# Copying two output banks on two engines, and moving one batch's side work to other steps, in an attention-then-MLP kernel

## The chip, the cores and the metric

The kernel runs on one core of one Trainium2 chip. The metric is the device time of one execution in microseconds; a time is given as the median of several executions.

## The reference, cut to what matters

```
def _attn_ref(q, k, v, agents):
    a2k = sm(agents, k)          # softmax over the 12480 keys, 49 agents
    agent_v = a2k @ v
    q2a = sm(q, agents)          # softmax over the 49 agents
    return q2a @ agent_v

def _moe_ref(x, w_in, w_out):
    h = x @ w_in                 # 128 -> 2048
    g = np.maximum(0.01 * h, h)  # leaky relu
    return g @ w_out             # 2048 -> 128
```

There are two batches of 12480 tokens with 128 channels, and all 24960 rows pass through the MLP.

## The kernel before, in words

The sums over the keys and values give a small matrix per batch; its product with `w_in` is folded into the tiles `m_hi` and `m_lo`, so that a token's 49 attention weights lead straight to its 2048 hidden values. The leaky relu is written as 0.99 times a relu plus a linear part, which the products with `l_hi` and `l_lo` carry. Every factor is split in a rounded high part and a low rest, to reach float32 accuracy with three products.

**Blocks and steps.** Tokens are worked in 52 blocks of 480 (26 for each batch). A block has 8 steps, f = 0 to 7, one for each pair of hidden tiles. In a step TensorE makes `mm1` (L739, 6 matmuls of 64 rows into an `h` pair of banks; there are two such pairs), ScalarE and VectorE make the relu's parts `hi` (L759) and `lo` (L760), and two steps later (`LAG`) TensorE makes `mm2` (L766, 12 matmuls) into the two output banks `o[0]` and `o[1]` of the block. Matmuls of 64 rows run in two halves of the array side by side: rows 0 to 63 go to `o[0]`, rows 64 to 127 to `o[1]`.

**The turnover.** There is one set of output banks. The last `mm2` of block i-1 stands in step f = 1 of block i, and the first one of block i in step f = 2. In between `o_copy` (L794) brings both banks to SBUF; GpSimd adds the two copies and SyncE stores the block (`o_add`, L808). `o_copy` stands at the beginning of step f = 2, ahead of that step's `mm1`.

**Side work.** Other work is hung onto steps by a table: `at(step, fn, ...)` puts a function behind the `relu` of a step, ahead of its `mm2`. Each engine works through its own instructions in the order in which the program issues them, so the table sets the queues. Two kinds matter here.

- The attention weights of a later block, by `chain` (L820): `q_half` (L614, products `aux<-qhi` and `aux<-qlo` at f = 1 and f = 2), `q_sum` at f = 0 on VectorE (tile `sm`), `q_swap` at f = 0 on GpSimd (two copies that exchange halves of `sm`), `q_rec` at f = 1 on VectorE (three instructions into `rs`, L696 to L703), `q_norm` at f = 1 on GpSimd.
- The second batch's sums, during the first batch's blocks. `k_score` and `k_keep` (scores and running maximum) at f = 5 of blocks 0 to 6; then `k_max0` to `k_max3` (the maximum over the tile, turned by TensorE and spread again); then for each half chunk of values `k_vhi` (VectorE rounds the values into `vr`), `k_vlo`, `k_ehi`, `k_elo`, and for each two of them `k_av2` (L438: 16 matmuls into a bank pair `aux`, then two VectorE additions into `avs`). There are 13 calls of `k_av2`, in blocks 9 to 21. The pair `aux` is a single buffer (`ps_x`, L140) that `k_score`, `k_max1`, `k_av2`, `q_half` and the products for `m_hi` share. At the end `fin`, `f_parts`, `w_parts`, `k_m2` and `k_m` make `m_hi` and `m_lo` of the second batch.

The main loop and the two functions that the change cuts apart are printed here.

Of the kernel before, what the change touches and what calls it, by code (L numbers as in the profile page):

```python
# [8 lines left out]
F32 = mybir.dt.float32  # L9
# [54 lines left out]
def tile_agent_attention_then_leaky_mlp(  # L64
# [27 lines left out]
    nc = tc.nc  # L92
# [7 lines left out]
    NB = G * TP  # L100
# [14 lines left out]
    LAG = 2  # L115
    NP = NF // 2
# [31 lines left out]
    def halves(name):  # L148

        return [ps_o.tile([P, MC], F32, tag=f"o{g}", name=f"{name}{g}") for g in range(2)]  # L150

    def pair(name):
        return ps_h.tile([P, 2, MC], F32, tag="h", name=name)
# [356 lines left out]
    fin = f_add, f_den, f_tr, f_avT, f_rec  # L510
# [223 lines left out]
                nc.sync.dma_start(out=t[o:o + SL], in_=t[x:x + SL])  # L734


    h_t, r_t, o_t = {}, {}, {}

    def mm1(i, p):  # L739

        b = i // BPB
        ps = pair("h")
        t = pT_t[i]
        for n, (w, x) in enumerate(((m_hi, 0), (m_hi, 1), (m_lo, 0))):
            for g, r in enumerate(ROWS):
                nc.tensor.matmul(  # L746
                    ps[:, g, :NB], lhsT=w[b][r, cols(2 * p + g)], rhs=t[r, x],
                    start=(n == 0), stop=(n == 2),
                )
        h_t[i, p] = ps  # L750

    def cols(f):
        return slice(f * P, (f + 1) * P)

    def relu(i, p):
        ps = h_t.pop((i, p))[:, :, :NB]
        hi = rp.tile([P, 2, NB], F32R, tag="hi", name="hi")
        lo = rp.tile([P, 2, NB], F32R, tag="lo", name="lo")
        nc.scalar.activation(hi, ps, AF.Relu)  # L759
        nc.vector.scalar_tensor_tensor(  # L760
            out=lo, in0=ps, scalar=0.0, in1=hi.bitcast(F32),
            op0=ALU.max, op1=ALU.subtract,
        )
        r_t[i, p] = (hi, lo)

    def mm2(i, p):  # L766

        b = i // BPB
        if p == 0:
            o_t[i] = halves("o")  # L770
        o = o_t[i]
        hi, lo = r_t.pop((i, p))

        def add(w, x, start=False, stop=False):
            for g, r in enumerate(ROWS):
                nc.tensor.matmul(o[g][:, :NB], lhsT=w[r], rhs=x[r], start=start, stop=stop)  # L776

        for g in range(2):
            f = 2 * p + g
            add(wo_hi[:, f, :], hi[:, g], start=(f == 0))  # L780
            add(wo_lo[:, f, :], hi[:, g])
        if p == NP // 2:
            t = pT_t[i]
            for w, x, g in ((l_hi, 0, 0), (l_lo, 0, 1), (l_hi, 1, 0)):
                g ^= i % 2 == 0
                r = ROWS[g]
                nc.tensor.matmul(  # L787
                    o[g][:, :NB], lhsT=w[b][r], rhs=t[r, x], start=False, stop=False
                )
        for g in range(2):  # L790
            f = 2 * p + g
            add(wo_hi[:, f, :], lo[:, g], stop=(f == NF - 1))

    def o_copy(i):  # L794
        t = p1.tile([P, 2, NB], F32, tag="oT", name="oT")
        o = o_t.pop(i)
        if i < NBLK - 1:
            for g in range(2):
                nc.scalar.copy(t[:, g], o[g][:, :NB])  # L799
            x_t["o"] = t  # L800
            return
        h = NB // 2
        for c, eng in ((slice(0, h), nc.sync), (slice(h, NB), nc.scalar)):
            nc.scalar.copy(t[:, 1, c], o[1][:, c])
            nc.vector.tensor_tensor(out=t[:, 0, c], in0=o[0][:, c], in1=t[:, 1, c], op=ALU.add)
            eng.dma_start(out=out[:, i * NB + c.start:i * NB + c.stop], in_=t[:, 0, c])
# [9 lines left out]
    def at(step, fn, *a):  # L816
        side.setdefault(step, []).append((fn, a))
# [21 lines left out]
    for b in range(1, B):  # L839
        i0 = (b - 1) * BPB  # L840

        n0 = NP * i0 + 5
        for c in range(NCH):
            s = n0 + c // 2 * NP
            if c == 0:
                at(s - 5, load_k, b, 0)
                at(s - 5, load_k, b, 1)
            if c + 2 < NCH:
                at(s - 1, load_k, b, c + 2)
            at(s, k_score, b, c, 0)  # L850
            at(s, k_score, b, c, 1)
            if c % 2:
                at(s, k_keep, b, c - 1)
            if c % 2 or c == NCH - 1:
                at(s, k_keep, b, c)
        n0 += (NCH - 1) // 2 * NP
        for p, fn in ((1, k_max0), (3, k_max1), (3, k_max1d), (7, k_max2), (7, k_max3)):
            at(n0 + p, fn, b)
        n0 += NP
        lag = 7  # L860
        for h in range(NH):
            s = n0 + h * NP // 2
            if h % 2 == 0:
                c = h // 2
                at(s - 5, load_v, b, c)
                at(s, k_sub, b, c, nc.gpsimd)
                at(s + 2, k_exp, b, c)
            at(s + 3, k_ehi, b, h, h, nc.scalar)
            at(s + 3, k_elo, b, h, h, nc.gpsimd)
            at(s + 1, k_vhi, b, h, h, nc.vector)  # L870
            at(s + 2, k_vlo, b, h, h, nc.gpsimd)
            if h % 2:
                at(s + lag, k_av2, b, h // 2)
        n0 += (NH - 1) * NP // 2 + lag
        for p, fn in zip((1, 5, 5, 5, 5), fin):
            at(n0 + p, fn, b)
        at(n0 + 7, f_parts, b)
        for m in range(0, NM, 2):
            s = n0 + 5 + (m // 2 + 1) * NP
            at(s - 4, w_parts, b, m)  # L880
            at(s - 2, w_parts, b, m + 1)
            at(s, k_m2, b, m)
        at(s + NP, k_m, b, NM)

    with tc.manual_schedule():
# [28 lines left out]
        for o, a, n in SLOTS:  # L914
            nc.vector.tensor_tensor(
                out=sel[:, o:o + n], in0=ident[:EW, a:a + n],
                in1=ident[:EW, HALF + a:HALF + a + n], op=ALU.add,
# [10 lines left out]
        for what, c in loads:  # L928
            fn, cost = fetch[what]
# [17 lines left out]
        for n in range(2 * NM):  # L947
# [11 lines left out]
            if n % 2 == 0:  # L959
                m = n // 2  # L960
# [54 lines left out]
        steps = [(i, p) for i in range(NBLK) for p in range(NP)]  # L1015
        for s in range(len(steps) + LAG):
            if s < len(steps):
                i, f = steps[s]
                if i > 0 and f == LAG:
                    o_copy(i - 1)  # L1020
                mm1(*steps[s])
                relu(*steps[s])
                for fn, a in side.get(s, ()):
                    fn(*a)
            if s >= LAG:
                mm2(*steps[s - LAG])
        o_copy(NBLK - 1)


# [37 lines left out]
```

## Time and profile before

| | |
|---|---|
| median of 3 executions | 996.9 us (996.54 to 997.06) |
| the profiled execution, its own time | 997.26 us |
| its span, first to last instruction | 995.4 us |
| TensorE matmul busy | 970.8 us, 98% |
| VectorE busy | 735.8 us, 74% |
| ScalarE busy | 616.3 us, 62% |
| GpSimd busy | 385.7 us, 39% |
| granted TensorE clock | full in all 40 slices (2.4 GHz) |

A TensorE that is busy 98% of the span isn't working 98% of it: the end of a matmul is modelled, so one that waits between two others can look like a long one. What a step costs is read from the distance between the same instruction in successive steps or blocks.

### The profile page before, as it was taken

The page shows a single profiled execution, that of the slowest core. Times are in us where ns is not written, and L with a number is a line of the kernel's source. Part 1 is how long each engine was busy: PE and PEld are TensorE (multiplying, and loading weights), DVE is VectorE, ACT ScalarE, POOL GpSimd, SP SyncE. Part 2 cuts the span into 40 slices and gives each one's busy share as a digit, 9 for nine tenths or more (in the row PEclk, how much of TensorE's full clock was granted, in tenths as well). Part 3 has the DMA queues.
Part 4 walks back from the last instruction along what each step waited for, and adds up shares of the span by engine and source line. Part 5 has one row for each costly group of instructions (what it writes and reads, how often), then busy time and mean ns, then how long its engine had stood idle before and what let it go on. Part 6 is the DMA issues. An engine that isn't in the chain of part 4 may idle for free.

```text
span 995.4 us, 23015 instructions
## 1 busy us (share of the span) xinstructions
PE 970.8 (98%) x9438; PEld 838.4 (84%) x9438; DVE 735.8 (74%) x1071; ACT 616.3 (62%) x907; POOL 385.7 (39%) x561
## 2 busy tenths in 40 slices
PE   8889999999999999999999999999999999999998
PEld 6768888888888888888888888888888888888887
DVE  7967677678778778777777677767777777777774
ACT  5755666666666656655666666666666666666654
POOL 2113233345655655653433333333333333333320
PEclk9999999999999999999999999999999999999999
DMA  9931322312312312311111111111111111212110
GB/s 347 372 119 32 111 71 90 81 51 72 81 50 71 82 51 71 81 32 51 41 30 51 41 51 40 51 41 51 41 44 47 42 50 31 60 32 61 31 40 21
DMA packets 28836, 70.01 MB, mean 70 GB/s; under 512 B 4387, under 2 KB 17955, under 8 KB 28731
## 3 DMA queue, kind: packets, MB, share of 16 engines
q1 hardware_dynamic: 28587, 68.42, 22.7%
q8 instruction: 74, 1.21, 0.5%
q14 instruction: 31, 0.25, 0.1%
q10 hardware_dynamic: 144, 0.12, 0.0%
HBM read 43.46 MB, written 12.78 MB: 57 GB/s over the span
## 4 chain that ended last, share of the span: by engine, by line
PE 89%; DVE 5%; ACT 2%; DMA 2%; issue 1%; POOL 1%; SPq 0%; DVEq 0%; POOLq 0%; ACTq 0%
PE o L776 54%; PE h L746 27%; PE aux L620 3%; DVE lo L760 2%; ACT hi L759 2%; PE o L787 1%; PE aux L353 1%; DVE avs L453 1%; PE sc L353 1%; DMA kt<-in_k_dram 1%; DMA vt<-in_v_dram 1%; PE avw L469 1%; DVE sm L688 1%; PE avw L302 0%; PE mp L535 0%
## 5 line engine op out<-in xcount | busy, mean ns | idle before, releaser
L760 DVE SCALAR_TENSOR_TENSOR lo<-h,hi 128x960 fp32r<-128x960 f32 x416 | 481.1, 1157 | 229.3 <-ACT hi L759 215.1
L759 ACT ACTIVATE hi<-h 128x960 fp32r<-128x960 f32 x416 | 405.6, 975 | 297.7 <-PE h L746 288.8
L776 PE MATMUL o<-hi,wo_hi 64*128 64x480 f32 x1664 | 426.6, 384 | 0.0
L776 PE MATMUL o<-hi,wo_lo 64*128 64x480 f32 x1664 | 413.7, 379 | 0.0
L746 PE MATMUL h<-pT,m_hi 64*128 64x480 f32 x1664 | 330.5, 377 | 1.0 <-POOL pT L319 0.8
L776 PE MATMUL o<-lo,wo_hi 64*128 64x480 f32 x1664 | 328.8, 375 | 0.0
L776 PEld LDWEIGHTS o<-hi,wo_hi 64*128 64x128 f32 x1664 | 260.1, 184 | 34.1 <-ACT oT L799 14.0
L776 PEld LDWEIGHTS o<-hi,wo_lo 64*128 64x128 f32 x1664 | 259.0, 184 | 17.7
L746 PEld LDWEIGHTS h<-pT,m_hi 64*128 64x128 f32 x1664 | 226.6, 184 | 21.1 <-POOL pT L319 1.1
L776 PEld LDWEIGHTS o<-lo,wo_hi 64*128 64x128 f32 x1664 | 227.3, 184 | 19.6
L746 PE MATMUL h<-pT,m_lo 64*128 64x480 f32 x832 | 235.3, 375 | 0.0
L746 PEld LDWEIGHTS h<-pT,m_lo 64*128 64x128 f32 x832 | 134.7, 184 | 12.7
L319 POOL TENSOR_TENSOR pT<-pt,pT 64x480 fp32r<-64x480 f32 (+1 forms) x52 | 63.6, 1223 | 147.0 <-ACT pT L722 147.0
L665 POOL COPY sm<-sm 32x15 f32<-32x15 f32 (+1 forms) x52 | 9.8, 189 | 189.0 <-DVE sm L688 189.0
L319 POOL TENSOR_TENSOR qlo<-qt,qhi 128x480 fp32r<-128x480 f32 x52 | 64.0, 1231 | 46.3 <-ACT qhi L583 45.2
L708 POOL TENSOR_TENSOR pd<-d,rs 64x375 f32<-64x375 f32 (+1 forms) x52 | 42.5, 818 | 92.1 <-DVE rs L703 86.1
L799 ACT COPY oT<-o 128x480 f32<-128x480 f32 x102 | 52.1, 563 | 29.1 <-PE o L776 29.1
L810 POOL TENSOR_TENSOR oT<-oT 128x480 f32<-128x480 f32 x51 | 62.4, 1223 | 9.8 <-issue 9.8
L319 POOL TENSOR_TENSOR d<-st,mm 64x375 f32<-64x375 f32 (+1 forms) x52 | 44.4, 854 | 49.0 <-DVE mm L671 47.8
L620 PE MATMUL aux<-qhi,a_hl 64*128 64x240 f32 x200 | 39.9, 284 | 10.1 <-DVE avs L453 8.2
L319 POOL TENSOR_TENSOR vr<-vt,vr 120x512 fp32r<-120x512 f32 x26 | 33.9, 1302 | 32.6 <-DVE vr L314 30.4
L620 PEld LDWEIGHTS aux<-qhi,a_hl 64*128 64x128 f32 x200 | 27.6, 184 | 17.5 <-issue 14.1
(139 smaller groups left out, 873.0 us busy)
## 6 DMA issues: line engine op xcount, KB each, us to landing
qt<-in_q_dram SPq DMA_DIRECT2D x53, 240.0 KB, 2.7
kt<-in_k_dram SPq DMA_DIRECT2D x26, 480.0 KB, 7.9
out_dram<-oT SPq DMA_DIRECT2D x51, 240.0 KB, 2.0
pT<-pT SPq DMA_DIRECT2D x100, 120.0 KB, 2.3
vt<-in_v_dram SPq DMA_DIRECT2D x13, 520.0 KB, 8.2
vt<-in_v_dram SPq DMA_DIRECT2D x13, 487.5 KB, 4.4
w<-in_w_in_dram SPq DMA_DIRECT2D x4, 512.0 KB, 7.3
w<-in_w_out_dram SPq DMA_DIRECT2D x4, 512.0 KB, 8.1
```

What stands on the lines that cost most here:

```text
L319: eng.tensor_tensor(out=o, in0=x, in1=y, op=ALU.subtract)
L353: nc.tensor.matmul(ps[r, j * NA:(j + 1) * NA], lhsT=k_t[b, c][:, j, r], rhs=a_sb[:, b, :], start=True, stop=True,)
L453: nc.vector.tensor_tensor(out=av_t[b], in0=ps[:EW, g, :VW], in1=av_t[b], op=ALU.add)
L469: nc.tensor.matmul(av_t[b][o:o + NA], lhsT=s_sb[:, c, j, :], rhs=v_t[b, c][:TP, j, :], start=False, stop=False,)
L620: nc.tensor.matmul(s_t[i][:, m, :h], lhsT=a_hl[i // BPB][r], rhs=x[r, m * h:(m + 1) * h], start=(s == 0 and n == 0), stop=(n == 1), skip_g ...
L708: nc.gpsimd.tensor_tensor(out=pd[:n, :, :A0], in0=d[:n], in1=w[:n].to_broadcast([n, NT, A0]), op=ALU.mult,)
L746: nc.tensor.matmul(ps[:, g, :NB], lhsT=w[b][r, cols(2 * p + g)], rhs=t[r, x], start=(n == 0), stop=(n == 2),)
L759: nc.scalar.activation(hi, ps, AF.Relu)
L760: nc.vector.scalar_tensor_tensor(out=lo, in0=ps, scalar=0.0, in1=hi.bitcast(F32), op0=ALU.max, op1=ALU.subtract,)
L776: nc.tensor.matmul(o[g][:, :NB], lhsT=w[r], rhs=x[r], start=start, stop=stop)
L799: nc.scalar.copy(t[:, g], o[g][:, :NB])
L810: nc.gpsimd.tensor_tensor(out=t[:, 0], in0=t[:, 0], in1=t[:, 1], op=ALU.add)
```

## The change

The relu is cut in two: `relu` keeps the ScalarE part, the new `rest` makes VectorE's `lo`. In seven steps of a block `rest` follows `relu` at once, as before. In step f = 1 of every block but the first (`turnover`) it comes last: after the side work and after the last `mm2` of the block before, the two output banks are copied, `o[0]` by ScalarE and `o[1]` by VectorE, and then `rest` is issued. The values of the second batch begin 6 steps later, the turned maximum (`k_max1`, `k_max1d`) one step earlier, and what closes the batch is spaced to stay at its old places within a block.

```
     def relu(i, p):
         ...
         nc.scalar.activation(hi, ps, AF.Relu)
+        r_t[i, p] = (hi, lo)
+        l_t[i, p] = ps
+
+    def rest(i, p):
+        hi, lo = r_t[i, p]
         nc.vector.scalar_tensor_tensor(
-            out=lo, in0=ps, scalar=0.0, in1=hi.bitcast(F32),
+            out=lo, in0=l_t.pop((i, p)), scalar=0.0, in1=hi.bitcast(F32),
             op0=ALU.max, op1=ALU.subtract,
         )
-        r_t[i, p] = (hi, lo)
...
         if i < NBLK - 1:
-            for g in range(2):
-                nc.scalar.copy(t[:, g], o[g][:, :NB])
+            nc.scalar.copy(t[:, 0], o[0][:, :NB])
+            nc.vector.tensor_copy(t[:, 1], o[1][:, :NB])
...
-        for p, fn in ((1, k_max0), (3, k_max1), (3, k_max1d), (7, k_max2), (7, k_max3)):
+        for p, fn in ((1, k_max0), (2, k_max1), (2, k_max1d), (7, k_max2), (7, k_max3)):
             at(n0 + p, fn, b)
-        n0 += NP
+        n0 += NP + 6
...
-        for p, fn in zip((1, 5, 5, 5, 5), fin):
+        for p, fn in zip((1, 7, 7, 7, 7), fin):
             at(n0 + p, fn, b)
-        at(n0 + 7, f_parts, b)
+        at(n0 + 9, f_parts, b)
         for m in range(0, NM, 2):
-            s = n0 + 5 + (m // 2 + 1) * NP
+            s = n0 + 7 + (m // 2 + 1) * NP
...
             if s < len(steps):
                 i, f = steps[s]
-                if i > 0 and f == LAG:
-                    o_copy(i - 1)
-                mm1(*steps[s])
-                relu(*steps[s])
+                turnover = i > 0 and f == LAG - 1
+                mm1(i, f)
+                relu(i, f)
+                if not turnover:
+                    rest(i, f)
                 for fn, a in side.get(s, ()):
                     fn(*a)
             if s >= LAG:
                 mm2(*steps[s - LAG])
+            if s < len(steps) and turnover:
+                o_copy(i - 1)
+                rest(i, f)
         o_copy(NBLK - 1)
```

Within a block `k_av2` thereby moves from f = 0 to f = 6 of the same block, `k_vhi` from f = 2 and 6 to f = 0 and 4, `k_ehi` and `k_elo` from f = 0 and 4 to f = 2 and 6, `k_sub` and `k_exp` from f = 5 and 7 to f = 3 and 5.

VectorE's queue at a turnover of the second batch's blocks, where no values are summed. Here is the order before; `sm` is made at f = 0, `rs` at f = 1, and the `lo` between them belongs to f = 1:

```order
707 L688 TENSOR_REDUCE sm<-d 64x15
708 L760 SCALAR_TENSOR_TENSOR lo<-h,hi 128x960
709 L696 SCALAR_TENSOR_TENSOR rs<-sm 64x15
710 L700 TENSOR_TENSOR rs<-rs,d 64x15
711 L703 RECIPROCAL rs<-rs 64x15
712 L760 SCALAR_TENSOR_TENSOR lo<-h,hi 128x960
713 L716 STREAM_TRANSPOSE pt<-pd 64x480
```

And the same place in the changed kernel:

```order
709 L688 TENSOR_REDUCE sm<-d 64x15
710 L696 SCALAR_TENSOR_TENSOR rs<-sm 64x15
711 L700 TENSOR_TENSOR rs<-rs,d 64x15
712 L703 RECIPROCAL rs<-rs 64x15
713 L803 COPY oT<-o_9906 128x480
714 L765 SCALAR_TENSOR_TENSOR lo<-h,hi 128x960 x2
715 L716 STREAM_TRANSPOSE pt<-pd 64x480
```

The bank's copy (L803) stands behind the three `rs` instructions and ahead of `lo` of f = 1, which has moved behind `rs` and the copy and now stands next to `lo` of f = 2.

VectorE's queue at the same place of a block in which values are summed, before (`avs` are the two additions of `k_av2`, `vr` the rounding of `k_vhi`):

```order
280 L688 TENSOR_REDUCE sm<-d 64x15
281 L453 TENSOR_TENSOR avs<-aux,avs 113x258 x2
282 L760 SCALAR_TENSOR_TENSOR lo<-h,hi 128x960
283 L696 SCALAR_TENSOR_TENSOR rs<-sm 64x15
284 L700 TENSOR_TENSOR rs<-rs,d 64x15
285 L703 RECIPROCAL rs<-rs 64x15
286 L760 SCALAR_TENSOR_TENSOR lo<-h,hi 128x960
287 L716 STREAM_TRANSPOSE pt<-pd 64x480
288 L646 TENSOR_TENSOR sq<-aux,sx 64x480
289 L314 CAST vr_114<-vt 120x4x128
```

And now:

```order
294 L453 TENSOR_TENSOR avs<-aux,avs 113x258 x2
295 L765 SCALAR_TENSOR_TENSOR lo<-h,hi 128x960 x2
296 L688 TENSOR_REDUCE sm<-d 64x15
297 L314 CAST vr_114<-vt 120x4x128
298 L696 SCALAR_TENSOR_TENSOR rs<-sm 64x15
299 L700 TENSOR_TENSOR rs<-rs,d 64x15
300 L703 RECIPROCAL rs<-rs 64x15
301 L803 COPY oT<-o_3710 128x480
302 L765 SCALAR_TENSOR_TENSOR lo<-h,hi 128x960 x2
```

The additions have left f = 0 and stand two `lo` earlier, behind `lo` of f = 6; a rounding of values has come between `sm` and `rs`.

## Rows read from the trace of the kernel before

**Rows 1.** The page, part 1: engine, busy us (share of the span), instructions.
```profile
PE 970.8 (98%) x9438; PEld 838.4 (84%) x9438; DVE 735.8 (74%) x1071; ACT 616.3 (62%) x907; POOL 385.7 (39%) x561
```

**Rows 2.** Waits, all engines: who waited <- for whom: us, times, longest.
```profile
PEld aux L620 <- issue: 14.1, 14, 1.0
PEld o L776 <- ACT oT L799: 14.0, 53, 0.4
...
PE aux L620 <- DVE avs L453: 8.2, 13, 0.6
```

**Rows 3.** Timeline, ScalarE, blocks 11, 13 and 37: start us, us, instruction [idle before].
```profile
277.49 1.02 ACT L799 COPY oT<-o 128x480 f32<-128x480 f32 x2 [1.12 <-PE o L776]
...
315.12 1.02 ACT L799 COPY oT<-o 128x480 f32<-128x480 f32 x2 [1.11 <-PE o L776]
...
740.80 1.02 ACT L799 COPY oT<-o 128x480 f32<-128x480 f32 x2 [0.29 <-PE o L776]
```

**Rows 4.** Timeline, all engines, block 11, steps f = 0 and 1.
```profile
271.54 0.40 PE L445 MATMUL aux<-vr,er 64*113 64x258 f32 x2
...
272.54 0.39 PE L776 MATMUL o<-hi,wo_hi 64*128 64x480 f32 x1
...
274.67 0.87 DVE L453 TENSOR_TENSOR avs<-aux,avs 113x258 f32<-113x258 f32 x2
...
275.68 0.38 PE L620 MATMUL aux<-qhi,a_hl 64*128 64x240 f32 x2 [0.63 <-DVE avs L453]
```

**Rows 5.** Timeline, all engines, block 35, steps f = 0 to 3.
```profile
704.87 1.16 DVE L760 SCALAR_TENSOR_TENSOR lo<-h,hi 128x960 fp32r<-128x960 f32 x1 [0.79 <-ACT hi L759]
...
705.94 0.51 DVE L688 TENSOR_REDUCE sm<-d 64x15 f32<-64x360 f32 x1
...
706.59 0.19 POOL L665 COPY sm<-sm 32x15 f32<-32x15 f32 x1 [4.26 <-DVE sm L688]
...
706.82 0.19 POOL L666 COPY sm<-sm 32x15 f32<-32x15 f32 x1
706.83 1.16 DVE L760 SCALAR_TENSOR_TENSOR lo<-h,hi 128x960 fp32r<-128x960 f32 x1 [0.37 <-ACT hi L759]
...
707.14 1.02 ACT L799 COPY oT<-o 128x480 f32<-128x480 f32 x2 [0.29 <-PE o L776]
...
707.75 0.48 PE L776 MATMUL o<-hi,wo_hi 64*128 64x480 f32 x1
...
707.91 0.15 DVE L696 SCALAR_TENSOR_TENSOR rs<-sm 64x15 f32<-64x15 f32 x1
...
708.21 0.48 PE L776 MATMUL o<-hi,wo_hi 64*128 64x480 f32 x1
...
708.31 0.24 DVE L703 RECIPROCAL rs<-rs 64x15 f32<-64x15 f32 x1
...
709.41 0.80 PE L746 MATMUL h<-pT,m_hi 64*128 64x480 f32 x4
```

**Rows 6.** Timeline, GpSimd and ScalarE, block 34, the same place.
```profile
689.79 0.19 POOL L666 COPY sm<-sm 32x15 f32<-32x15 f32 x1
...
690.31 1.02 ACT L799 COPY oT<-o 128x480 f32<-128x480 f32 x2 [0.49 <-PE o L776]
```

**Rows 7.** Groups of VectorE instructions by shape: count | busy us, mean ns | idle before.
```profile
L362 DVE COPY run<-aux 120x392 f32<-120x392 f32 x1 | 0.5, 544 | 0.0
```

**Rows 8.** The tile vr: count: duration ns min/median/max, first and last start us.
```profile
L314 DVE CAST vr<-vt x26: 398/939/1498, 215.2 to 450.9; 120x512 fp32r<-120x512 f32 x26
```

**Rows 9.** Timeline, GpSimd and VectorE, block 10, steps f = 6 and 7.
```profile
269.91 1.22 POOL L319 TENSOR_TENSOR qlo<-qt,qhi 128x480 fp32r<-128x480 f32 x1
269.94 1.48 DVE L314 CAST vr<-vt 120x512 fp32r<-120x512 f32 x1
```

**Rows 10.** Timeline, VectorE and TensorE, blocks 6 and 7, around the maximum.
```profile
196.52 0.59 PE L746 MATMUL h<-pT,m_lo 64*128 64x480 f32 x2
...
196.89 0.86 DVE L378 TENSOR_REDUCE rm<-run 120x49 f32<-120x392 f32 x1
```

More of the change, by code (lines that the diff above doesn't have):

```diff
@@ L734, in p_dup @@
                 nc.sync.dma_start(out=t[o:o + SL], in_=t[x:x + SL])
-    h_t, r_t, o_t = {}, {}, {}
+    h_t, r_t, l_t, o_t = {}, {}, {}, {}
     def mm1(i, p):
```

## The prediction

> **What bounds the kernel now.** The shares of busy time [rows 1] say TensorE, with room on the other three engines, but a busy TensorE may be waiting under its modelled ends, so the second view is the list of waits, and the third the distance between like instructions. The waits [rows 2] name two things that hold TensorE and that the change touches. The first product of `mm2` waits for ScalarE's output copy: 14.0 us over 53 times, 0.27 us a turnover. The attention products `q_half` wait for the bank pair `aux`: 14 times about 1.0 us, put down to "issue" on the weight loads (14.1 us) and to the additions `avs` on the matmuls (8.2 us, the same stalls seen later). 13 calls of `k_av2` and one turned maximum make those 14.
>
> The block length says the same without modelled ends. In the later blocks the output copies of blocks 35 and 37 lie (740.80 - 707.14) / 2 = 16.83 us a block apart [rows 3, 5]; in the blocks with values, 11 and 13, (315.12 - 277.49) / 2 = 18.82 us [rows 3]. The matmuls of `k_av2` themselves fill 271.54 to 272.54, 1.0 us [rows 4]. So 18.82 - 16.83 - 1.0 = 0.99 us of such a block is stall, 13 times.
>
> **Why that stall exists, and the first term.** In block 11 the additions ended at 274.67 + 0.87 = 275.54, and `q_half` began at 275.68 [rows 4]. The additions come so late because they stand behind `sm` in VectorE's queue. The change puts `k_av2` at f = 6 and its additions behind `lo` of f = 6; `q_half` needs the pair at f = 1 of the next block, three steps of 706.83 - 704.87 = 1.96 us later [rows 5]. Additions of 0.87 us [rows 4] fit there, since a step's own VectorE work is one `lo` of 1.16 us [rows 5] and the step with `k_av2` is 1.0 us longer. **Saved: 13 x 0.99 = 12.9 us.** The matmuls only move. The copies and rounding on ScalarE and GpSimd that move with them land in steps where these engines idle (62% and 39% busy, [rows 1]).
>
> **The turned maximum: nothing.** Its stall at `q_half`, the 14th, goes, but a new one comes: `k_max1` turns `rm`, which VectorE has at 196.89 + 0.86 = 197.75, and one step earlier TensorE would reach it after the last `mm1` matmul of that step, issued from 196.52, at about 196.75 [rows 10]. A wait of 1.0 us takes the place of one of 1.0 us.
>
> **The turnover, 51 times.** Here the words of the change promise most, and I expect next to nothing. The second bank was copied behind the first on ScalarE; now VectorE takes it, but VectorE is not free. Ahead of its copy stand the three `rs`, and they need what GpSimd's second `sm` copy writes. Block 35 by its rows [rows 5]:
> - `lo` of f = 0 ends at 706.03, `sm` at 706.45, GpSimd's copies run from 706.59 to 706.82 + 0.19 = 707.01. All of this hangs on TensorE's `mm1` and stays.
> - `rs`: before, it waited behind `lo` and took from 707.91 to 708.31 + 0.24 = 708.55, 0.64 us. Now it starts at 707.04 and ends at 707.68. (A hand-over takes 0.14 us from `sm` to GpSimd; where VectorE follows an engine that it waits for I take 0.03, and 0.14 as the far bound.)
> - The copy of 480 columns from PSUM has no row on VectorE. The nearest is 544 ns for 392 columns [rows 7]; `lo`, which reads 960 columns of PSUM in 1.16 us, gives (1160 - 544) / (960 - 392) = 1.08 ns a column, so 88 columns more make 0.64 us. An instruction may begin 0.09 us before the one ahead ends, as `sm` does behind `lo`. So it runs from 707.60 or 707.68 to 708.24 or 708.32.
> - Before, ScalarE's two copies ended at 707.14 + 1.02 = 708.16 and the waiting product came at 708.21 [rows 5]. Now it comes **0.08 to 0.16 us later**.
>
> Blocks alternate, because one of the array's halves carries one matmul more in even blocks and the other in odd ones. In block 34 GpSimd's second copy ends at 689.98 and ScalarE's two at 691.33 [rows 6]; the same sum (0.03 + 0.64 - 0.08 or 0 + 0.64) gives 691.21 to 691.29, **0.04 to 0.12 us earlier**. The mean over a pair of blocks is +0.02 us (-0.02 to +0.06): 51 x 0.02 = **1.0 us lost**, bounds -1 to +3.
>
> **A rounding of values between `sm` and `rs`, 13 times.** With no neighbour it takes 398 ns; beside a GpSimd instruction up to 1498 [rows 8], as when `qlo` started 0.03 us ahead of it and it ended 0.29 us after `qlo` had [rows 9]. Behind `sm` it would run from 706.37 to 706.77 in block 35's times, while GpSimd's `sm` copy wants to start at 706.59. If the two exclude each other and the earlier goes first, the copies and all behind them move by 706.77 - 706.59 = 0.18 us: 13 x 0.18 = **2.3 us lost**. If they don't, nothing is lost; if GpSimd goes first, the rounding is done 0.40 us after 707.01 and `rs` starts 0.37 us late, 4.8 us. I take the first.
> The Trainium skill (SBUF — State Buffer, Who interferes with whom) has that rule: VectorE in its two-port modes and GpSimd lock each other out of a shared port pair, and the one that issues first keeps it for the whole instruction. The trace agrees as far as the 398 and 1498 ns go; that VectorE can hold up GpSimd in turn no row here shows. Without the rule this term would be 0 and the sum 2.3 us lower.
>
> **The `h` banks: nothing, by a thin margin.** `lo` of f = 1 now follows the copy, and `mm1` of f = 3 needs its bank. It ends 1.16 - 0.09 = 1.07 us after the copy and TensorE's hand-over takes 0.05 (708.16 to 708.21): 1.12. That `mm1` came 709.41 - 708.16 = 1.25 us after the copies' end [rows 5]. The margin is 0.13 us; without overlap, and with a hand-over of 0.14, 0.05 us would be missing, 51 x 0.05 = 2.6 us, the far bound. ScalarE, relieved of 0.46 us a block, waits for `mm1` and gives nothing.
>
> **Sum.** -12.9 + 1.0 + 2.3 = -9.6 us on the profiled execution's 997.26 us gives 987.7. That execution stands 0.36 us above the median of 996.9, so I predict **987.3 us**. Best bound: -12.9 - 1 = -13.9, 983.0. Worst: -12.9 + 3 + 4.8 + 2.6 = -2.5, 994.4.
>
> **Rivals.**
> - *The turnover opens fully* (chance 0.10): VectorE begins its copy with ScalarE's, at 707.14, and the product comes at about 707.83, no later than its own turn. A block's matmuls alone need 8 x 1.96, two times about 0.22 for `q_half`, and 0.33 for the linear part's three half-array matmuls, 16.45 us, against 16.83: 0.38 us a turnover, 19 us. With the first term 996.9 - 12.9 - 19 = **965 us**. For it: the 14.0 us in the waits. Against: `rs` has begun right behind whatever stood ahead of it, never out of turn, and its inputs come at 707.01 [rows 5]. The Trainium skill (PSUM — Partial Sum Buffer, Specifications) says that ScalarE and VectorE can read PSUM at full rate together if their banks differ, as here; no row of before shows the two reading output banks at once, and the rule doesn't speak of what stands ahead in the queue.
> - *VectorE becomes the turnover's last engine by more than I count* (chance 0.06), the slower side. Bank `o[1]` and the `h` pair now both hang on GpSimd's `sm` copies. If these start x later than 706.59, TensorE loses x at each turnover; from x = 12.9 / 51 = 0.25 us on, the first term is eaten. At 0.35 us it gives 996.9 - 12.9 + 18 = **1002 us**. For it: GpSimd's work for the values now lies around f = 5 to 2. Against: it sat idle 4.26 us before that copy [rows 5], and 38 of the 51 blocks have no such work.
> - *The stall only moves* (chance 0.06): the bank pair is still late, now for `k_av2` at f = 6 or for the step behind its additions. About **997 us**. Against: `q_half`'s readers work at f = 2, four steps ahead.
>
> **How the numbers follow.** The forecast gets 0.78, the rivals 0.10, 0.06 and 0.06. Its bounds are 983.0 to 994.4; I give 981 to 995, which adds a turnover that gains a little (0.04 us each) and leaves out the rivals. A measurement of this kernel tells about 0.2%, 2 us, from no change. Faster by more than that are the forecast and the first rival, less a little for its worst bound: 0.87. Within 0.2%: 0.07. Slower: 0.06.
>
> **What would show it.** Right: the wait of `q_half` for `avs` and its 14.1 us are gone; blocks with values last 17.8 to 18.1 us and later blocks 16.8 to 16.9; `rs` starts within 0.1 us of GpSimd's second `sm` copy and VectorE's copy of `o[1]` behind it takes about 0.64 us; TensorE's wait at the turnover is now for that copy. Wrong: later blocks of 16.5 us (first rival) or over 17.05 (second); a rounding of values that doesn't delay `sm`'s copies (the 2.3 us); a wait of `mm1` of f = 3 for `lo` (the `h` banks).

## The result and the profile after

| | before | changed |
|---|---|---|
| median, same chip | 996.72 us (996.42 to 997.06, 4 executions) | 982.79 us (982.37 to 984.32, 4 executions) |
| the profiled execution, its span | 997.26, 995.4 us | 982.59, 980.8 us |

The ratio is 0.9863 (95% interval 0.9846 to 0.988): 13.9 us faster. The forecast was 987.3 us with a range of 981 to 995. Direction and main cause came out as forecast, but two terms of the sum were sized too dear, and a third, put at nothing, cost a little. Medians leave out the executions at a lower TensorE clock, which are one each of experiments 8 and 9 (1160 and 1422 us, mean granted clock 0.75 and 0.61 of full) and one of the kernel before beside them.

The changed kernel's page, part 1; it answers to [rows 1]:

```profile
PE 963.9 (98%) x9438; PEld 901.4 (92%) x9438; DVE 746.5 (76%) x1122; ACT 595.9 (61%) x856; POOL 384.3 (39%) x561
```

Its list of waits; it answers to [rows 2]:

```profile
DVE rs L696 <- POOL sm L666: 25.8, 50, 0.6
ACT oT L802 <- PE o L780: 19.0, 49, 0.5
...
PEld o L780 <- DVE oT L803: 9.2, 35, 0.4
```

The 14.1 us of weight loads for `q_half` and the 8.2 us put down to `avs` are gone. TensorE's wait at the turnover is still there, for VectorE's copy in place of ScalarE's, and VectorE itself now waits 50 times for GpSimd's second `sm` copy.

ScalarE's timeline, the copies of blocks 11, 13, 35 and 37; it answers to [rows 3]:

```profile
272.41 0.56 ACT L802 COPY oT<-o 128x480 f32<-128x480 f32 x1 [0.29 <-PE o L780]
...
308.14 0.56 ACT L802 COPY oT<-o 128x480 f32<-128x480 f32 x1 [0.29 <-PE o L780]
...
692.95 0.56 ACT L802 COPY oT<-o 128x480 f32<-128x480 f32 x1 [0.29 <-PE o L780]
...
726.54 0.56 ACT L802 COPY oT<-o 128x480 f32<-128x480 f32 x1 [0.29 <-PE o L780]
```

A block with values lasts (308.14 - 272.41) / 2 = 17.87 us, 0.95 less than before. A later block lasts (726.54 - 692.95) / 2 = 16.80 us, 0.03 less than before: there the copy on two engines gained next to nothing.

The turnover of block 35, all engines; it answers to [rows 5]:

```profile
691.76 0.51 DVE L688 TENSOR_REDUCE sm<-d 64x15 f32<-64x360 f32 x1
...
692.40 0.19 POOL L665 COPY sm<-sm 32x15 f32<-32x15 f32 x1 [4.26 <-DVE sm L688]
...
692.63 0.19 POOL L666 COPY sm<-sm 32x15 f32<-32x15 f32 x1
...
692.85 0.17 DVE L696 SCALAR_TENSOR_TENSOR rs<-sm 64x15 f32<-64x15 f32 x1 [0.58 <-POOL sm L666]
...
693.27 0.24 DVE L703 RECIPROCAL rs<-rs 64x15 f32<-64x15 f32 x1
...
693.44 0.58 DVE L803 COPY oT<-o 128x480 f32<-128x480 f32 x1
...
694.08 0.18 PEld L780 LDWEIGHTS o<-hi,wo_hi 64*128 64x128 f32 x1 [0.27 <-DVE oT L803]
```

The output banks are done at 692.95, as ScalarE's copy shows, but VectorE's copy begins 0.49 us later, behind the three `rs`. These begin 0.03 us after GpSimd's second copy has ended (692.63 + 0.19 = 692.82), as the prediction had it.

### The profile page after: what moved, and what is told of

Read it like the earlier page. It is cut to its first block, busy times and chain, and to the rows that moved or that the text cites. A ratio compares the mean times of both kernels' runs of the same rounds, so it can differ in the third digit from the quotient of the medians.

```text
span 980.8 us, 23077 instructions
## 1 busy us (share of the span) xinstructions
PE 963.9 (98%) x9438; PEld 901.4 (92%) x9438; DVE 746.5 (76%) x1122; ACT 595.9 (61%) x856; POOL 384.3 (39%) x561
## 4 chain that ended last, share of the span: by engine, by line
PE 83%; DVE 8%; ACT 3%; issue 2%; DMA 2%; POOL 1%; SPq 0%; POOLq 0%; DVEq 0%; ACTq 0%
PE o L780 50%; PE h L746 24%; DVE lo L765 3%; ACT hi L759 3%; PE o L791 2%; DVE oT L803 1%; PE aux L620 1%; PE aux L445 1%; PE aux L353 1%; DVE sm L688 1%; PE sc L353 1%; DMA kt<-in_k_dram 1%; DMA vt<-in_v_dram 1%; PE avw L469 1%; DVE rs L700 1%
## 5 line engine op out<-in xcount | busy, mean ns | idle before, releaser
L765 DVE SCALAR_TENSOR_TENSOR lo<-h,hi 128x960 fp32r<-128x960 f32 x416 | 475.5, 1152 | 177.7 <-ACT hi L759 174.4
L780 PEld LDWEIGHTS o<-hi,wo_lo 64*128 64x128 f32 x1664 | 262.3, 184 | 5.9
L780 PEld LDWEIGHTS o<-lo,wo_hi 64*128 64x128 f32 x1664 | 235.5, 184 | 9.3
L746 PEld LDWEIGHTS h<-pT,m_hi 64*128 64x128 f32 x1664 | 230.8, 184 | 7.8 <-POOL pT L319 1.1
L746 PEld LDWEIGHTS h<-pT,m_lo 64*128 64x128 f32 x832 | 137.0, 184 | 2.9
L620 PE MATMUL aux<-qhi,a_hl 64*128 64x240 f32 x200 | 43.0, 271 | 1.4 <-ACT hi L759 1.4
L620 PE MATMUL aux<-qlo,a_hl 64*128 64x240 f32 x200 | 43.2, 272 | 0.0
L802 ACT COPY oT<-o 128x480 f32<-128x480 f32 x51 | 28.6, 561 | 19.0 <-PE o L780 19.0
L654 DVE STREAM_TRANSPOSE st<-sq 64x480 f32<-64x480 f32 (+1 forms) x52 | 34.3, 660 | 0.0
```

Source lines behind the costliest of these rows:

```text
L620: nc.tensor.matmul(s_t[i][:, m, :h], lhsT=a_hl[i // BPB][r], rhs=x[r, m * h:(m + 1) * h], start=(s == 0 and n == 0), stop=(n == 1), skip_g ...
L654: nc.vector.transpose(t[:n].rearrange("p n a -> p (n a)"), s_t[i][:n])
L746: nc.tensor.matmul(ps[:, g, :NB], lhsT=w[b][r, cols(2 * p + g)], rhs=t[r, x], start=(n == 0), stop=(n == 2),)
L765: nc.vector.scalar_tensor_tensor(out=lo, in0=l_t.pop((i, p)), scalar=0.0, in1=hi.bitcast(F32), op0=ALU.max, op1=ALU.subtract,)
L802: nc.scalar.copy(t[:, 0], o[0][:, :NB])
```

## The experiments

The theory after the result: the moved steps take the stall of `q_half` away, and that is nearly all; the copy on two engines would free the banks some 0.4 us earlier, but the three `rs` ahead of it in VectorE's queue wait for GpSimd and eat that up. The rival: the two parts share the gain, or the turnover is bound by something else than that queue. One execution of a kernel can differ from another of the same kernel by 1 to 3 us (experiment 2: 991.54 to 994.6), much of it in the first two blocks, which the profiled executions finish between 102.6 and 105.1 us though only one turnover lies there; the medians of the kernel before, measured beside each set of experiments, lie between 996.72 and 997.28. Where less matters, block lengths are compared. A block length without a row beside it is the mean over blocks 27 to 50 (later blocks) or 10 to 20 (values; in the kernel before and in experiment 2, block 21 has work in it that closes the batch), by the mean start of the six `mm1` matmuls of f = 0; by that measure before has 16.82 and 18.81, the changed kernel 16.80 and 17.86.

**1. The moves alone** (the kernel before with the changed table of steps):

```
-        for p, fn in (... (3, k_max1), (3, k_max1d), ...):
+        for p, fn in (... (2, k_max1), (2, k_max1d), ...):
-        n0 += NP
+        n0 += NP + 6
```

> The second batch's steps moved, the output copies and the relu as before. My theory (the gain is the wait of the attention products for the bank pair, 13 times 0.99 us, and the turnover is worth next to nothing): -12.5 to -13.5 us against before, 983.2 to 984.4 us; no wait of q_half for avs; later blocks 16.83 us, blocks with values 17.8 us. Rival (the gain comes from the copies on two engines, 0.27 us or more at each of 51 turnovers): 0 to -3 us, 994 us or more.

Measured: 984.33 us, ratio 0.987 (0.9857 to 0.9884), 12.85 us less than before (997.18 in those executions). The list of waits has ScalarE's copy where it was [rows 2], and nothing of `avs`:

```profile
PEld o L776 <- ACT oT L799: 13.5, 53, 0.4
```

Later blocks keep 16.82 us, blocks with values have 17.84. From f = 0 of block 9 to f = 0 of block 26, by the same measure, the stretch shrinks from 317.87 to 304.82 us, by 13.0. The moves are nearly the whole of the change.

**2. The copies alone** (the changed kernel with the table of steps of before):

```
-        n0 += NP + 6
+        n0 += NP
```

> The output copies on two engines and the relu part behind them, the second batch's steps as before. My theory: within 2 us of before (995 to 998.5), the 14 waits of about 1.0 us of q_half for avs still there, in the blocks with values too, and later blocks 16.80 us. Rival (copies on two engines are what gains): 983 to 986 us.

Measured: 992.49 us, ratio 0.9953 (0.9941 to 0.9965): 4.7 us less than before. Both sides missed. The timeline of block 11, VectorE, TensorE and ScalarE, shows why:

```profile
275.64 0.87 DVE L453 TENSOR_TENSOR avs<-aux,avs 113x258 f32<-113x258 f32 x2
...
276.63 0.22 PEld L620 LDWEIGHTS aux<-qhi,a_hl 64*128 64x128 f32 x2 [1.01 <-issue]
...
277.23 0.24 DVE L703 RECIPROCAL rs<-rs 64x15 f32<-64x15 f32 x1
...
278.46 0.56 ACT L802 COPY oT<-o 128x480 f32<-128x480 f32 x1 [1.11 <-PE o L780]
278.50 0.66 DVE L803 COPY oT<-o 128x480 f32<-128x480 f32 x1 [1.03 <-PE o L780]
```

`q_half` still waits a microsecond for the additions, and in that microsecond VectorE finishes the `rs` (277.47, a microsecond ahead of the banks). Here its copy does begin with ScalarE's, and a block with values shrinks from 18.81 to 18.53 us: 13 x 0.28 = 3.6 us. The later blocks shrink by 0.02. So the parts don't add up: alone they bring 12.85 and 4.7, together 13.9, since the stall that the moves remove was the cover under which the copies gained.

**3. `rs` behind the copy** (the changed kernel; in the turnover's step `q_rec` and `q_norm` are issued last):

```
+                late = (q_rec, q_norm) if turnover else ()
                 for fn, a in side.get(s, ()):
-                    fn(*a)
+                    if fn not in late:
+                        fn(*a)
...
                 o_copy(i - 1)
                 rest(i, f)
+                for fn, a in side.get(s, ()):
+                    if fn in late:
+                        fn(*a)
```

> The changed kernel with q_rec (three rs instructions on VectorE) and q_norm of the turnover's step issued behind the copy and lo, so that VectorE's copy no longer stands behind an instruction that waits for GpSimd. My theory (VectorE's copy is late only because of rs): the copy starts 0.1 us after ScalarE's, TensorE gets its bank 0.2 to 0.35 us earlier at 51 turnovers, -10 to -18 us against the changed kernel: 965 to 973 us; later blocks 16.45 to 16.6 us. Rival (the h bank, held by lo behind the copy, or the product's own turn sets the turnover): within 4 us of the changed kernel, 979 to 983 us.

Measured: 972.37 us, ratio 0.9749 (0.9736 to 0.9763), 10.4 us less than the changed kernel: the version that beats both. The timeline of block 34, ScalarE, VectorE and TensorE's weight loads:

```profile
669.98 0.56 ACT L802 COPY oT<-o 128x480 f32<-128x480 f32 x1 [0.49 <-PE o L780]
670.02 0.66 DVE L803 COPY oT<-o 128x480 f32<-128x480 f32 x1 [0.92 <-PE o L780]
...
670.59 1.15 DVE L765 SCALAR_TENSOR_TENSOR lo<-h,hi 128x960 fp32r<-128x960 f32 x1
...
671.66 0.16 DVE L696 SCALAR_TENSOR_TENSOR rs<-sm 64x15 f32<-64x15 f32 x1
...
671.85 0.48 PEld L746 LDWEIGHTS h<-pT,m_hi 64*128 64x128 f32 x4
```

Both copies begin together, TensorE's wait for VectorE's copy is gone from the list of waits, the later blocks last 16.60 us, those with values 17.62. The late `rs` cost GpSimd a wait (120.3 us over 51 times for `pd`), which hardly anybody waits for in turn (VectorE's transposition, 0.9 us in all).

**4. GpSimd's copies twice** (the changed kernel, `q_swap` issued twice at f = 0):

```
             at(max(NP * n + r, 0), fn, n)
+            if (r, fn) == (-8, q_swap):
+                at(max(NP * n + r, 0), fn, n)
```

> The changed kernel with GpSimd's two sm copies issued twice (50 blocks), 0.42 to 0.45 us more before rs may start; GpSimd has idle time for it. My theory (TensorE's turnover hangs on GpSimd's sm copies through rs and VectorE's copy): 0.42 us more at each turnover, +18 to +22 us against the changed kernel, 1001 to 1005 us, slower than before the change. Rival (GpSimd has slack there): 982 to 986 us.

Measured: 1008.43 us, ratio 1.0114 (1.0099 to 1.013), 25.6 us more than the changed kernel and more than the 18 to 22 expected. The list of waits:

```profile
DVE rs L696 <- POOL sm L666: 51.4, 50, 1.2
...
PEld o L780 <- DVE oT L803: 36.7, 50, 0.9
```

The later blocks last 17.31 us, 0.52 more, as much as two more GpSimd copies 0.25 us apart; the expectation had 0.42 for the two. In the changed kernel a turnover pays for every delay of `sm` one to one. That is the second rival's chain: it is real, only nothing pulled on it.

**5. `rs` between copy and `lo`** (as 3, with the two calls one place further up):

```
                 o_copy(i - 1)
+                for fn, a in side.get(s, ()):
+                    if fn in late:
+                        fn(*a)
                 rest(i, f)
```

> The changed kernel with the three rs instructions between VectorE's copy of o[1] and the delayed lo of f = 1 (order: copy, rs, lo; in e3_rs_behind it is copy, lo, rs). Output banks are free as early as in e3. Theory A (the h banks bind: mm1 of f = 3 waits for lo of f = 1, which in e3 left it about 0.05 us): lo ends about 0.57 us later, TensorE loses about 0.5 us at each of 51 turnovers against e3's 972.4, so 995 to 1000 us, slower than the changed kernel too. Rival B (lo has slack, only the output banks decide): 971 to 976 us.

Measured: 999.67 us, ratio 1.0028 (1.0018 to 1.0037): 27.3 us more than experiment 3. One wait of its list and, from its timeline of block 34, VectorE's `lo` of f = 1 and 2 and the load that waits for the first:

```profile
PEld h L746 <- issue: 30.2, 50, 1.2
...
690.52 2.15 DVE L765 SCALAR_TENSOR_TENSOR lo<-h,hi 128x960 fp32r<-128x960 f32 x2
...
691.72 0.33 PEld L746 LDWEIGHTS h<-pT,m_hi 64*128 64x128 f32 x4 [0.48 <-issue]
```

The output banks come as early as in 3, yet it is slower than the kernel before: the `h` banks hang on `lo` of f = 1. The first of the two `lo` ends at 691.60 by its own record, and the load comes 0.116 us later. Later blocks last 17.04 us (0.44 more than in 3), those with values 18.44 (0.82 more). Block 14, GpSimd and VectorE, shows where the latter lose the other 0.38:

```profile
330.32 1.30 POOL L319 TENSOR_TENSOR vr<-vt,vr 120x512 fp32r<-120x512 f32 x1
...
331.13 0.52 DVE L696 SCALAR_TENSOR_TENSOR rs<-sm 64x15 f32<-64x15 f32 x1
```

Beside GpSimd's subtraction for `vr`, which began first, the first `rs` takes 0.52 us, where it takes 0.16 in block 34, and ends 0.03 us after the subtraction (331.65 and 331.62). `lo` and the load come later by that.

**6. One engine again** (as 3, with both copies on ScalarE):

```
-            nc.vector.tensor_copy(t[:, 1], o[1][:, :NB])
+            nc.scalar.copy(t[:, 1], o[1][:, :NB])
```

> e3_rs_behind with both banks copied by ScalarE again, lo still behind nothing but the side work, rs behind lo. Theory A (with rs out of the way the two engines in parallel are what frees the banks in time): the second bank comes about 0.4 us later, the turnover costs what it cost before, later blocks about 16.83 us, 983 to 986 us. Rival B (the place of the copy ahead of the step's other work is what gains, one engine would do): 971 to 976 us.

Measured: 983.97 us, ratio 0.9867 (0.985 to 0.9883). Its waits and its timeline show the old picture [rows 2, 3], with blocks of (727.49 - 693.83) / 2 = 16.83 us:

```profile
PEld o L780 <- ACT oT L803: 12.9, 51, 0.3
...
693.83 0.56 ACT L802 COPY oT<-o 128x480 f32<-128x480 f32 x1 [0.29 <-PE o L780]
...
727.49 0.56 ACT L802 COPY oT<-o 128x480 f32<-128x480 f32 x1 [0.29 <-PE o L780]
```

With the moves in place, the four corners are:

| | `rs` where it stood | `rs` behind copy and `lo` |
|---|---|---|
| ScalarE copies both banks | 984.3 (experiment 1) | 984.0 (experiment 6) |
| ScalarE and VectorE, one each | 982.8 (the changed kernel) | 972.4 (experiment 3) |

Neither the second engine nor the place of `rs` is worth 2 us by itself; together they are worth 12. (In experiment 1 `lo` of f = 1, too, stands where it stood, ahead of `rs`; in the other three it stands behind the copy.)

**7. The rounding out of the way** (the changed kernel; `k_vhi` one step earlier, so that it leaves the place between `sm` and `rs`):

```
-            at(s + 1, k_vhi, b, h, h, nc.vector)
+            at(s, k_vhi, b, h, h, nc.vector)
```

> The changed kernel with the rounding of values one step earlier (f = 7 and 3 in place of f = 0 and 4), so that it stands ahead of lo of f = 0 and no longer between sm and rs. Theory A (the rounding holds GpSimd's first sm copy up by about 0.07 and rs by about 0.09 us in 13 turnovers, as the trace of the changed kernel suggests): about 1.1 us less, 981.3 to 982.1 us. Rival B (the recorded size, 0.18 us each): 980.4 us. Rival C (no cost, or one that moves to lo of f = 0): 982.8 us or more.

Measured: 982.82 us, ratio 0.9857 (0.9843 to 0.9872). The whole time shows nothing, as rival C had it. The blocks do: those with values last 17.80 us in place of 17.86, 13 x 0.06 = 0.8 us; in this profiled execution the first two blocks took 0.7 us longer than in the one of the changed kernel. Block 14, VectorE and GpSimd, in the changed kernel:

```profile
324.73 0.51 DVE L688 TENSOR_REDUCE sm<-d 64x15 f32<-64x360 f32 x1
325.16 0.41 DVE L314 CAST vr<-vt 120x512 fp32r<-120x512 f32 x1
325.37 0.25 POOL L665 COPY sm<-sm 32x15 f32<-32x15 f32 x1 [3.64 <-DVE sm L688]
...
325.67 0.19 POOL L666 COPY sm<-sm 32x15 f32<-32x15 f32 x1
325.89 0.17 DVE L696 SCALAR_TENSOR_TENSOR rs<-sm 64x15 f32<-64x15 f32 x1 [0.32 <-POOL sm L666]
```

and in this experiment:

```profile
325.16 0.51 DVE L688 TENSOR_REDUCE sm<-d 64x15 f32<-64x360 f32 x1
325.81 0.19 POOL L665 COPY sm<-sm 32x15 f32<-32x15 f32 x1 [3.63 <-DVE sm L688]
326.04 0.19 POOL L666 COPY sm<-sm 32x15 f32<-32x15 f32 x1
326.26 0.17 DVE L696 SCALAR_TENSOR_TENSOR rs<-sm 64x15 f32<-64x15 f32 x1 [0.59 <-POOL sm L666]
```

Beside the rounding GpSimd's first copy takes 0.25 us in place of 0.19, and `rs` starts 1.16 us after `sm` does in place of 1.10.

**8 and 9. Half of `lo`** (the changed kernel, and experiment 3, with `lo` of f = 1 made for one of two hidden tiles):

```
+        n = 1 if i > 0 and p == LAG - 1 else 2
         nc.vector.scalar_tensor_tensor(
-            out=lo, in0=l_t.pop((i, p)), scalar=0.0, in1=hi.bitcast(F32),
+            out=lo[:, :n], in0=l_t.pop((i, p))[:, :n], scalar=0.0, in1=hi.bitcast(F32)[:, :n],
...
-            add(wo_hi[:, f, :], lo[:, g], stop=(f == NF - 1))
+            add(wo_hi[:, f, :], lo[:, 0 if i > 0 and p == LAG - 1 else g], stop=(f == NF - 1))
```

> The changed kernel with lo of f = 1 made for the first of its two hidden tiles only (480 columns instead of 960), so that lo ends about 0.5 us earlier; mm2 of that step uses the first tile's lo for both, so the second tile's low part is left out of the result. In the changed kernel the first weight load of mm1 of f = 3 comes 0.116 us after that lo's end in every later block, and 1.18 us after the copy's end where before it came 1.02 to 1.04 after; but two steps later only 0.03 us of the 0.14 are left. Theory A (the h banks hold the weight loads up, which costs 0.03 us a turnover): the load comes 1.02 to 1.05 us after the copy's end, 1.5 us less in all, 981.0 to 981.7 us. Rival B (the 0.14 cost in full): 975 to 977 us. Rival C (no wait there, 0.116 is chance): the load stays where it is, 982.3 to 983.3 us.

> e3_rs_behind (972.4 us) with the same half lo at f = 1, the second tile's low part left out of the result. There too the first weight load of mm1 of f = 3 comes 0.116 us after lo's end, and the load of the step behind stands 3.09 and 3.03 us behind the copy's end in even and odd blocks, against 2.99 before. Theory A (the h banks are part of the 0.17 us a block that e3 still stands above its matmuls): 0.10 and 0.04 us less, mean 0.07, so 968 to 970 us, later blocks 16.52 to 16.55. Rival B (the rest is VectorE's copy of o[1] alone): 971.8 to 973 us.

Measured: 982.48 us, ratio 0.9853 (0.9837 to 0.9869), for the changed kernel with half a `lo`, and 971.44 us, ratio 0.9744 (0.973 to 0.9758), for experiment 3 with it. Block 35, VectorE and the weight loads, of 8:

```profile
693.51 0.58 DVE L804 COPY oT<-o 128x480 f32<-128x480 f32 x1
...
694.02 0.63 DVE L766 SCALAR_TENSOR_TENSOR lo<-h,hi 128x480 fp32r<-128x480 f32 x1
...
695.13 0.18 PEld L746 LDWEIGHTS h<-pT,m_hi 64*128 64x128 f32 x1
```

and of the changed kernel, from two windows:

```profile
693.95 1.13 DVE L765 SCALAR_TENSOR_TENSOR lo<-h,hi 128x960 fp32r<-128x960 f32 x1
...
695.20 0.47 PEld L746 LDWEIGHTS h<-pT,m_hi 64*128 64x128 f32 x4
```

Behind the copy's end the load comes after 695.13 - 694.09 = 1.04 us with half a `lo`, and after 695.20 - 694.02 = 1.18 us with the whole one, which ends 0.12 us ahead of the load. So in the changed kernel the `h` banks do hold the load up, by 0.14 us at a turnover, and rival C of 8 falls, though the whole time lies in its range. But the later blocks gain only 0.016 us (16.798 to 16.782), and 0.022 in experiment 9 (16.597 to 16.575): about 0.8 and 1.1 us in all, half and a third of what theory A expected, and the time of experiment 9 lies between its two ranges. A weight load runs ahead of its matmuls, and most of its delay was that lead. Experiment 3 stands 0.15 us a block above its matmuls alone (16.60 to the prediction's estimate of 16.45); what the 0.13 are that the `h` banks don't explain stays open.

## Why the prediction was right, and where it was not

- **The stall of `q_half`, -12.9 us: right.** Experiment 1 has 13.0 us less in blocks 9 to 25. The additions now end 3.8 us before the next `q_half` (284.78 and 288.62 us in block 11 and 12).
- **The turned maximum, nothing: right.** From block 6 to 8 the stretch is 53.65 us before and 53.63 in experiment 1, whose list of waits has the new one, 1.1 us at the product of `k_max1`.
- **The turnover, +1.0 us: the mechanism right, the size and sign wrong.** From the end of GpSimd's second copy to the end of the output copies block 35 took 708.16 - 707.01 = 1.15 us before [rows 5], and now 694.02 - 692.82 = 1.20; block 34 took 691.33 - 689.98 = 1.35 before [rows 6], and now 677.12 - 675.92 = 1.20, by these rows of the changed kernel's timeline, GpSimd and VectorE:

```profile
675.73 0.19 POOL L666 COPY sm<-sm 32x15 f32<-32x15 f32 x1
...
676.54 0.58 DVE L803 COPY oT<-o 128x480 f32<-128x480 f32 x1
```

  That is +0.05 and -0.15, where the prediction had +0.08 to +0.16 and -0.04 to -0.12. The step that failed is VectorE's copy at 0.64 us, pieced together from two other instructions: in the queue behind `rs` it takes 0.58. The mean is -0.05 a turnover in place of +0.02, about -2.6 us.
- **The `h` banks, nothing by a margin of 0.13 us: the price nearly right, its reason wrong.** The prediction measured the margin at the first `mm1` matmul. That one does come on time: 695.27 - 694.02 = 1.25 us behind the copies' end, as in [rows 5]. But `lo` holds up its weight load, which before came 709.20 - 708.16 = 1.04 us behind that end and had no margin even by the prediction's 1.12; now it comes 1.18 behind, since after `lo` the hand-over takes 0.116 us, not the 0.05 taken from ScalarE's copy. The first row is of the kernel before, the second of the changed one:

```profile
709.20 0.40 PEld L746 LDWEIGHTS h<-pT,m_hi 64*128 64x128 f32 x3
...
695.27 0.40 PE L746 MATMUL h<-pT,m_hi 64*128 64x480 f32 x1
```

  The load's lead over its matmul shrinks from 0.21 to 0.08 us, which by experiment 8 costs 0.8 us in all. Experiment 5 is what happens when the lead is used up.
- **The rounding between `sm` and `rs`, +2.3 us: right in kind, three times too dear.** It is 0.06 us a block, 0.8 us in all. The Trainium skill (SBUF — State Buffer, Who interferes with whom) says that the later of the two is blocked for the other's whole instruction; the prediction turned that into a start 0.18 us later. The trace agrees that GpSimd waits: its copy ends at 325.62, 0.05 us after the rounding's 325.57, and so it does in all 13 such blocks. But the wait doesn't add in full: a copy that began its 0.19 us only then would have ended at 325.76.
- **Sum.** Turnover (1.0 + 2.6), `h` banks (-0.8) and rounding (2.3 - 0.8) explain 4.3 of the 4.5 us between 987.3 and 982.8. The rest is less than executions differ.
- **The first rival** (the turnover opens fully, 965 us) fell for the reason that the prediction gave: `rs` never starts out of turn. Experiment 3 makes its condition true. Then the later blocks give 0.22 us (16.82 to 16.60), not the 0.38 of the rival. The Trainium skill (PSUM — Partial Sum Buffer, Specifications) has both engines reading PSUM at full rate if their banks differ. The trace agrees for ScalarE, whose copy takes 0.56 us beside VectorE's (669.98) as it does ahead of it (692.95); VectorE's takes 0.66 us there and 0.58 behind `rs`, on which see the last section. **The second rival**'s chain is shown by experiment 4 at its full price, but GpSimd's copies of `sm` came no later than before (in block 35 the second ends 692.82 - 691.76 = 1.06 us after `sm` starts, before 707.01 - 705.94 = 1.07), except by the 0.06 us in the 13 blocks with the rounding. **The third** fell with the waits for `avs`.

## What to carry to other kernels

Before giving a copy to a second engine, read what stands ahead of it in that engine's queue and whom that waits for: here three short instructions that wait for a third engine ate the whole gain, and issuing them two places later gave 10.4 us. Look also at what the copy pushes back: one place further up, the same three instructions made it slower than the kernel that had one engine copy all. And two edits that relieve the same stretch are not to be added up: a stall that one of them removes may be the cover of the other.

## What the runs showed of the hardware that was not expected

- VectorE's copy of 128 x 480 from PSUM takes 0.58 us where it begins behind a running instruction (693.44; 584 to 586 ns in nearly all turnovers of the changed kernel) and 0.66 where it begins from idle (670.02, 278.50). That ScalarE reads PSUM beside it is not the likelier reason: in experiment 4, where ScalarE's copy had ended before, and in the changed kernel's block 14, where the two overlap by 0.23 us, it takes 0.59 both times. In experiment 3 it begins from idle at every turnover and takes 0.66 every time, whether it begins 0.04 or 0.21 us behind ScalarE's.
- TensorE's first weight load comes 0.054 us after VectorE's copy ends, but 0.116 us after `lo` does, the same to 3 ns in every block looked at, in six kernels (the changed one and experiments 2 to 5 and 7). Why the two hand-overs differ was not tried.
- A weight load that comes 0.14 us late costs about 0.02 us a block (16.798 to 16.782 in experiment 8): its matmul still comes on time, 1.25 us behind the copies' end.
